# Convolutional attention and an expert layer on one core: idle transposes ahead of the first tokens, and the order of steps as a table

## The chip, the cores and the metric

The kernel runs on one core of a Trainium2 chip. The metric is the device time of one execution in microseconds (us); lower is better. The engines of the core are called PE (TensorE, the matrix engine; PEld is its loading of weights), DVE (VectorE), ACT (ScalarE), POOL (GpSimd) and SP (SyncE, which here only issues transfers). Each takes its instructions in program order.

## What is computed

Two stages on 33280 tokens of 192 numbers. First a causal convolution whose seven taps are a softmax per token and head:

```python
w = softmax(weight_gen)                       # [8, 4160, 8 heads, 7 taps]
x_unf = the last 7 rows of x for each token   # zeros ahead of the start
out = einsum('bshk,bskhg->bshg', w, x_unf)    # 8 heads x 24 numbers
```

Then an expert layer on the result `x` (33280 x 192), with `w_in` 192 x 1024 and `w_out` 1024 x 192:

```python
h = x @ w_in
solu = h * softmax(h)
ln = (solu - mean) / sqrt(var + 1e-6) * g_ln
return ln @ w_out
```

## The kernel before

**Tiling.** 33280 tokens are 128 partitions of 260 consecutive tokens. The kernel walks the 260 token indices t; one "tile" is the 128 tokens with the same t. x and the tap weights are loaded in chunks (token indices 0 to 3, 4 to 11, then 16 at a time).

**Steps.** The work is cut into 4199 named steps, each with the token index it works on. For one tile:

- POOL: `attA` (line 191) multiplies x by the tap weights for two tiles (up to token 11) or four tiles at once into the buffer `pr` (four buffers); `attB` (206) adds some of the seven products to each other; `t1` (109) and `t6` (122) prepare a chunk's tap weights together with `t0`, `t3`, `t5` on DVE (107, 115, 120) and `t2`, `t4` on ACT.
- The remaining parts are summed either by PE, which transposes each part and accumulates (`xT`, line 491, one buffer `pa`), or by DVE in `fin` (477), after which `xT` transposes the sum. The first twelve tiles leave all or nearly all parts to PE: 21 transposes per pair.
- `xhi` (ACT, 501) and `xld` (DVE, 505) copy the transposed pair out of `pa` as a high and a low half in f16; `sw` (SP, 511) makes a copy with the halves swapped.
- `mm1` (PE, 526 and 534) is the first product, six narrow pairs and six wide matmuls, into one of three buffers `h`. `max` (DVE, 556), `exp` (ACT, 562), `solu` (DVE, 570), `sq` (ACT, 576), `hi` (ACT, 583), `lo` (DVE, 587) work on it; `lo` is the last reader of `h`. `tr` (SP, 595) transposes the f16 halves by DMA.
- `mm2` (PE, 635) is the second product, 24 matmuls; `out` (ACT, 646) scales it, `od` stores four tiles. `f0` to `f5` make the layer norm's scale once per four tiles.

**Start-up.** The weights arrive as the two words of doubles. `a`, `b` steps turn `w_in` into f32 (lines 274 to 290), `c` steps `w_out`. `n0`, `n1`, `n2` (ACT, 328) sum the squares of `w_in`, `n4` (PE, 335) adds the sums over the partitions, `n6` and `n7` make a scale of it, `a03` to `b4` scale the weights into f16, and `w0` (SP, 307 to 311) copies them into a second arrangement for odd tiles; then `mm1` can start. `q` and `p` steps scale and centre `w_out` for `mm2` (`q.0` on POOL, 379; `p8` on DVE, 428). `v` steps make a norm of x per chunk. `x0` (248) masks the first rows, `lx` and `lw` load the chunks from the third on, `lx` in four parts.

**The idle products.** `pw` (`run_ahead`, 250 to 253) is PE's first step: 44 matmuls of fp32 ones with the first chunk of x, into `pa`, of which nothing is read. The `xT` of the first pair follows it on PE.

**The order.** `plan` lists each step with its engine, a cost and the steps that it waits for; `issue_order` then plays the plan engine by engine and at each turn takes the ready step with the smallest number, token index plus an entry of `URGENCY`. The instructions are written in that order, and each engine keeps it:

```python
for op, t in issue_order(plan(RUN, starts, group, stat_group, LOADS, parts)):
    ops[op](t)
```

Of the kernel before, what the change touches and what calls it, by code (L numbers as in the profile page):

```python
# [26 lines left out]
def tile_kernel(ctx: ExitStack, tc: tile.TileContext, x, weight_gen, w_in, w_out, g_ln, out):  # L27
    nc = tc.nc
    P = 128
# [95 lines left out]


# [123 lines left out]
    def run_ahead():  # L250
        pa = ps_a.tile([P, 3, P], F32, name="pa")
        for _ in range(AHEAD):
            nc.tensor.matmul(pa[:, 0, :D2], ones, xs[0][:, HALO * D : HALO * D + D2], start=True, stop=True)  # L253
# [109 lines left out]

# [234 lines left out]

# [100 lines left out]
    for op, t in issue_order(plan(RUN, starts, group, stat_group, LOADS, parts)):  # L699
        ops[op](t)  # L700

URGENCY = dict(
    a00=230.54, a01=-169.86, a02=78.81, a03=-71.26, a04=-52.3, a05=-245.39, a06=20.39, a10=-199.02,
    a11=183.38, a12=139.02, a13=75.55, a14=-236.05, a15=8.56, a16=-231.01, attA=(-80.23, 0, 0, 0),
    attA_0=93.55, attA_10=178.99, attA_2=-38.93, attA_4=125.32, attA_6=21.36, attA_8=6.86,
    attB=(58.83, 0, 0, 0), attB_0=40.66, attB_10=-53.52, attB_2=-167.73, attB_4=27.22, attB_6=-4.54,
    attB_8=126.24, b0=158.76, b1=-174.19, b2=200.95, b3=244.46, b4=-122.49, b5=232.43, b6=77.77,
    c00=-206.66, c01=-92.96, c02=162.77, c05=204.94, c06=-171.28, c10=-58.15, c11=-212.47,  # L710
    c12=49.83, c15=212.2, c16=242.46, c20=190.09, c21=97.28, c22=-4.95, c25=136.4, c26=-31.36,
    exp=(-145.96, -219.37, 18.21, 132.23), exp_0=197.26, exp_1=237.51, exp_10=83.17, exp_11=-194.86,
    exp_2=-108.44, exp_3=174.98, exp_4=36.04, exp_5=44.51, exp_6=-71.15, exp_7=57.6, exp_8=-99.33,
    exp_9=226.63, f0=(0, 0, 0, 153.51), f0_11=-38.19, f0_3=404.55, f0_7=96.61, f1=(0, 0, 0, 45.43),
    f1_11=224.73, f1_3=57.21, f1_7=-131.49, f2=(0, 0, 0, 256.79), f2_11=-171.14, f2_3=167.13,
    f2_7=-230.92, f3=(0, 0, 0, -162.74), f3_11=-141.49, f3_3=4.68, f3_7=-10.02, f4=(0, 0, 0, 5.77),
    f4_11=200.54, f4_3=174.19, f4_7=104.74, f5=(0, 0, 0, -199.21), f5_11=182.08, f5_3=193.17,
    f5_7=-182.31, fin=(115.66, 0, 69.89, 0), hi=(61.88, -187.14, -241.68, -119.88), hi_0=-28.29,
    hi_1=-69.46, hi_10=-154.42, hi_11=188.61, hi_2=234.68, hi_3=-165.38, hi_4=58.97, hi_5=32.18,
    hi_6=-155.21, hi_7=148.5, hi_8=53.7, hi_9=-126.75, lo=(-195.34, -225.17, -19.45, -178.56),  # L720
    lo_0=-73.26, lo_1=165.75, lo_10=-179.95, lo_11=-185.1, lo_2=-144.88, lo_3=-74.94, lo_4=228.22,
    lo_5=35.88, lo_6=-187.55, lo_7=-24.94, lo_8=-124.22, lo_9=-91.39, lw=-14.78, lx0=-135.21,
    lx1=125.55, lx2=223.55, lx3=-66.11, max=(-67.16, -31.06, -160.3, -253.27), max_0=-6.63,
    max_1=-109.95, max_10=-2.35, max_11=-181.02, max_2=-173.74, max_3=137.03, max_4=202.43,
    max_5=109.99, max_6=-231.43, max_7=-121.9, max_8=204.82, max_9=-131.88, mm1=(-241.67, -119.54,
    -126.73, 78.79), mm1_0=-129.22, mm1_1=194.49, mm1_10=216.67, mm1_11=108.18, mm1_2=-55.59,
    mm1_3=-173.16, mm1_4=-181.37, mm1_5=-116.52, mm1_6=99.99, mm1_7=119.82, mm1_8=-217.85,
    mm1_9=218.56, mm2=(-76.61, -1.63, 161.38, -206.56), mm2_0=59.48, mm2_1=-155.68, mm2_10=243.66,
    mm2_11=-207.18, mm2_2=-130.59, mm2_3=-13.88, mm2_4=40.87, mm2_5=-249.66, mm2_6=183.99,
    mm2_7=107.74, mm2_8=61.49, mm2_9=-113.27, n0=39.48, n1=53.35, n2=38.52, n4=201.04, n6=203.48,  # L730
    n7=-33.93, od=(0, 0, -76.55, -133.12), od_11=174.52, od_3=60.29, od_7=79.7, out=(-153.63, 6.11,
    53.99, -124.59), out_0=30.56, out_1=-87.51, out_10=-73.71, out_11=228.15, out_2=-278.7,
    out_3=212.6, out_4=2.25, out_5=-245.97, out_6=46.29, out_7=-69.48, out_8=-146.66, out_9=-22.02,
    p30=-79.19, p31=-243.38, p4=191.82, p5=174.62, p6=333.78, p70=25.49, p71=-226, p80=-73.8,
    p81=-140.51, p9=-85.22, pw=-76.84, q00=-128.77, q01=29.8, q02=27.49, q10=69.29, q11=242.54,
    q12=-155.16, q20=170.97, q21=339.47, q22=156.26, q30=228.51, q31=-227.09, q32=128,
    solu=(-199.24, -182.01, 8.5, -14.44), solu_0=129.39, solu_1=-56.22, solu_10=230.35,
    solu_11=-117.79, solu_2=99.72, solu_3=150.7, solu_4=-164.75, solu_5=118.7, solu_6=32.69,
    solu_7=-85.43, solu_8=22.47, solu_9=-24.22, sq=(81.8, -245.34, -58.76, 192.06), sq_0=192.25,
    sq_1=-73.99, sq_10=91.57, sq_11=62.94, sq_2=210.83, sq_3=7.36, sq_4=129.68, sq_5=-193.11,  # L740
    sq_6=-205.04, sq_7=-44.39, sq_8=-223.66, sq_9=-123.3, sw=(55.97, 0, 163.95, 0), sw_0=-167.4,
    sw_10=-118.23, sw_2=36.54, sw_4=39.41, sw_6=112.6, sw_8=-212.75, t0=271.79, t0_0=42.36,
    t0_4=216.57, t1=124.99, t1_0=-52.31, t1_4=-202.08, t2=245.01, t2_0=-82.33, t2_4=62.1, t3=136.26,
    t3_0=57.54, t3_4=69.25, t4=-31.14, t4_0=-142.07, t4_4=-84.48, t5=234.35, t5_0=-56.17,
    t5_4=-172.56, t6=94.73, t6_0=149.42, t6_4=97.15, tr=(-72.45, -45.15, 237.8, -222.84),
    tr_0=233.38, tr_1=48.73, tr_10=85.22, tr_11=40.86, tr_2=139.35, tr_3=109.02, tr_4=-170.49,
    tr_5=-176.28, tr_6=107.6, tr_7=43.11, tr_8=-31.21, tr_9=-152.72, v00=82.2, v00_0=198.87,
    v00_4=224.23, v01=218.42, v01_0=-245.65, v01_4=-75.77, v02=129.37, v03=233, v1=116.62,
    v1_0=-126.67, v1_4=-222.18, v2=226.63, v2_0=-231.41, v2_4=-20.17, v3=49.62, v3_0=-71.33,
    v3_4=35.56, v4=239.66, v4_0=-195.81, v4_4=113.57, v5=-56.74, v5_0=-173.27, v5_4=-127.37,  # L750
    w0=209.28, x0=-211.37, xT=(-87.23, 0, 53.04, 0), xT_0=77.08, xT_10=-226.06, xT_2=-99.19,
    xT_4=-107.64, xT_6=91.42, xT_8=-169.15, xhi=(-90.84, 0, -70.56, 0), xhi_0=165, xhi_10=188.48,
    xhi_2=152.35, xhi_4=-22.69, xhi_6=134.05, xhi_8=-231.09, xld=(44.29, 0, 58.42, 0), xld_0=-215.1,
    xld_10=-25.58, xld_2=124.15, xld_4=-166.69, xld_6=-122.65, xld_8=83.12,
)
# [18 lines left out]
LOADED = 20500  # L774
AHEAD = 44
CENTRED = 3
# [8 lines left out]
SUMS = {2: 880, 3: 1380, 4: 1840, 5: 2300}  # L785
LATER = dict(max=40, solu=35, mm1=0, mm2=95)


def plan(run, starts, group, stat_group, loads, parts):

    PE, DVE, ACT, SP, POOL = range(5)
    steps = []

    def add(name, t, engine, cost, *after, ready=0):
        steps.append((name, t, engine, cost, [x for x in after if x[1] >= 0], ready))

    def once(name, engine, cost, *after, ready=0):
        add(name, 0, engine, cost, *((x, 0) for x in after), ready=ready)

    def chunk_of(t):  # L800
        return max(c for c in range(len(starts) - 1) if starts[c] <= t)

    weights = dict(a0=8900, a1=10700, b=12500, c0=16200, c1=17500, c2=19200)
    order = list(weights)
    for n, part in enumerate(order):
        at = weights[part]
        sized = [order[n - 1] + "1"] if n else []
        if n > 3:
            sized.append(order[n - 4] + "2")
        once(part + "1", ACT, 620, *sized, ready=at)  # L810
        once(part + "0", DVE, 715, ready=at)
        once(part + "5", DVE, 715, part + "0")
        once(part + "6", DVE, 715, part + "5")
        once(part + "2", DVE, 700, part + "6", part + "1")
        if n < 3:
            once({"a0": "n0", "a1": "n1", "b": "n2"}[part], ACT, 830, part + "2")
            once(part + "3", ACT, 580, part + "2", "n7")
            once(part + "4", DVE, 660, part + "3")
    once("w0", SP, 3600, "a04", "a14", "b4")
    for f, part in enumerate(("c0", "c1", "c2", "c2")):  # L820
        made = (["c02"], ["c02", "c12"], ["c12", "c22"], ["c22"])[f]
        once(f"q{f}0", POOL, 830, *made, ready=16000)
        once(f"q{f}1", PE, 660, f"q{f}0", f"q{f - 1}1" if f else "c02")
        once(f"q{f}2", ACT, 520, f"q{f}0", "n4")
    for half, old in enumerate(centred_after()):
        add(f"p3{half}", 0, DVE, 900, ("q31", 0), ("mm1", CENTRED), *([("p30", 0)] if half else []), *old)
# [13 lines left out]
    def last_group(c):  # L840
        if c < 0:
            return ("attA", -1)
# [260 lines left out]
```

## Time and profile before

| | us |
|---|---|
| median of 3 runs | 1234.22 (1233.54 to 1234.49) |
| the profiled execution | 1234.71 |
| its span, first to last instruction | 1232.9 |
| PE, DVE, ACT, POOL busy | 1197.4, 1162.3, 1124.0, 1134.8 |

The profile is one execution. Its span lies 1.8 us below the execution's own time. A row of a timeline gives the start of a group of instructions, its length, engine, line, operation, what it writes and reads, and in brackets the idle time ahead of it with what ended it. Matmul ends are modelled, so neighbouring rows of PE overlap a little.

### The profile page before, as it was taken

The numbers are of one execution on the slowest core, as the hardware profiler recorded it, in microseconds if no ns is written. First come the engines' busy times: TensorE is split into PE (matmuls) and PEld (weight loads), VectorE is DVE, ScalarE is ACT, GpSimd is POOL, SyncE is SP. The second block draws the span as 40 slices with busy tenths as digits, with TensorE's granted clock in tenths as the row PEclk, the third lists the DMA queues.
The fourth block names the chain that finished last, engine by engine and source line by source line (L and its number), as shares of the span: only waits on it lengthen the run. The fifth ranks groups of instructions, "written<-read, shape, count | busy, mean of one in ns | idle before, by whom it ended". The sixth has DMA issues, their size and how long they took to land.

```text
span 1232.9 us, 27480 instructions
## 1 busy us (share of the span) xinstructions
PE 1197.4 (97%) x10303; PEld 829.2 (67%) x10303; DVE 1162.3 (94%) x1814; ACT 1124.0 (91%) x2295; POOL 1134.8 (92%) x243
## 2 busy tenths in 40 slices
PE   7899999999999999999999999999999999999998
PEld 7666666666666666666676666666666666666666
DVE  5989999999999999999999999999999999988994
ACT  4899898999899898999989999999999999999985
POOL 6689999999999999999999999999999999999930
PEclk9999999999999999999999999999999999999999
DMA  6787889989797988989698999979899897987786
GB/s 202 157 188 146 200 156 210 178 183 182 164 210 153 225 165 170 192 174 213 138 220 175 186 185 169 203 150 231 161 188 184 178 195 145 195 161 150 152 150 129
DMA packets 586069, 219.19 MB, mean 178 GB/s; under 512 B 548624, under 2 KB 566288, under 8 KB 585935
## 3 DMA queue, kind: packets, MB, share of 16 engines
q1 hardware_dynamic: 585776, 216.84, 86.1%
q8 instruction: 81, 1.33, 0.5%
q10 hardware_dynamic: 158, 0.59, 0.1%
q14 instruction: 54, 0.43, 0.1%
HBM read 46.19 MB, written 25.56 MB: 58 GB/s over the span
## 4 chain that ended last, share of the span: by engine, by line
ACT 35%; DVE 24%; PE 23%; issue 12%; DMA 5%; SPq 1%; ACTq 0%; DVEq 0%
ACT e L576 10%; PE po L635 9%; ACT hl L583 8%; ACT e L562 8%; DVE h L556 8%; PE h L534 7%; DVE h L570 6%; DVE hl L587 5%; PE h L526 4%; ACT junk L156 2%; DVE a L477 2%; ACT ot L646 2%; DMA xt<-in_x_dram 2%; PE pa L491 2%; PE pa L253 2%
## 5 line engine op out<-in xcount | busy, mean ns | idle before, releaser
L191 POOL TENSOR_TENSOR pr<-xt,wt 128x5376 f32<-128x5376 f32 (+1 forms) x68 | 631.3, 9284 | 0.9
L635 PEld LDWEIGHTS <-hlT 128*128 128x128 f16 x6240 | 522.5, 98 | 52.0 <-issue 7.9
L635 PE MATMUL po<-w_hl,hlT 128*128 128x192 f16 x6168 | 550.9, 246 | 5.5 <-ACT ot L646 5.4
L206 POOL TENSOR_TENSOR pr<-pr 128x2304 f32<-128x2304 f32 (+2 forms) x128 | 445.7, 3482 | 9.3
L570 DVE SCALAR_TENSOR_TENSOR h<-h,row,e 128x1024 f32<-128x1024 f32 x260 | 333.5, 1284 | 7.3 <-ACT e L562 4.2
L587 DVE SCALAR_TENSOR_TENSOR hl<-h,hl 128x1024 f16<-128x1024 f32 x260 | 311.3, 1216 | 28.0 <-ACT hl L583 17.1
L556 DVE TENSOR_SCALAR_CACHE_REDUCE h<-h,row 128x1024 f32<-128x1024 f32 x260 | 334.0, 1285 | 3.9 <-PE h L534 3.1
L562 ACT ACTIVATE e<-h,stats 128x1024 f32<-128x1024 f32 x260 | 294.9, 1134 | 38.2 <-DVE h L556 26.8
L576 ACT ACTIVATE e<-h,stats 128x1024 f32<-128x1024 f32 x260 | 294.4, 1134 | 30.3 <-DVE stats L607 24.9
L534 PEld LDWEIGHTS <-xh 128*128 128x128 f16 x1560 | 131.3, 98 | 234.5 <-issue 109.8
L583 ACT ACTIVATE hl<-h 128x1024 f16<-128x1024 f32 x260 | 268.7, 1034 | 4.8 <-DVE h L570 4.0
L534 PE MATMUL h<-wa,xh 128*128 128x512 f16 x780 | 190.9, 381 | 1.6 <-DVE wa L353 1.6
L534 PE MATMUL h<-oa,xh 128*128 128x512 f16 x780 | 191.0, 381 | 0.0
L646 ACT ACTIVATE ot<-po,stats 128x192 f32<-128x192 f32 x257 | 114.1, 444 | 5.1 <-PE po L635 4.6
L526 PE MATMUL h<-ob,turned 64*128 64x512 f16 x390 | 106.1, 378 | 10.3 <-DVE hl L587 9.1
L526 PE MATMUL h<-wb,xh 64*128 64x512 f16 x390 | 106.8, 380 | 3.6 <-DVE hl L587 3.0
L526 PE MATMUL h<-wb,turned 64*128 64x512 f16 x390 | 106.4, 380 | 0.8 <-DMA turned<-xh 0.8
L526 PE MATMUL h<-ob,xh 64*128 64x512 f16 x390 | 106.4, 380 | 0.6 <-DMA ob<-wa 0.6
L477 DVE TENSOR_REDUCE a<-pr 128x384 f32<-128x1152 f32 (+1 forms) x58 | 86.4, 1491 | 0.0
L491 PE MATMUL pa<-ident,pr 128*128 128x128 f32 x651 | 84.7, 276 | 1.4 <-DVE xh L505 1.2
L526 PEld LDWEIGHTS <-xh 64*128 64x128 f16 x780 | 53.6, 94 | 46.7 <-issue 24.7
L491 PEld LDWEIGHTS pa<-ident,pr 128*128 128x128 f32 x651 | 76.1, 143 | 12.8 <-issue 2.1
(91 smaller groups left out, 892.6 us busy)
## 6 DMA issues: line engine op xcount, KB each, us to landing
out_dram<-ot SPq DMA_DIRECT2D x64, 384.0 KB, 3.2
xt<-in_x_dram SPq DMA_DIRECT2D x30, 576.0 KB, 4.9
xt<-in_x_dram SPq DMA_DIRECT2D x30, 480.0 KB, 4.5
turned<-xh SPq DMA_DIRECT2D x260, 32.0 KB, 2.2
wt<-in_weight_gen_dram SPq DMA_DIRECT2D x15, 448.0 KB, 5.4
hlT<-hl SPq DMA_TRANSPOSE x260, 4.8
hlT<-in_moe_w_out_dram SPq DMA_DIRECT2D x3, 512.0 KB, 8.9
xt<-in_x_dram SPq DMA_DIRECT2D x3, 384.0 KB, 4.2
```

Of the source, the lines that this page charges most:

```text
L191: nc.gpsimd.tensor_tensor(out=window(pr, 0, [(ROW, K), (HG, n * H), (1, HG)]), in0=window(xt, t * D, [(D, K), (HG, n * H), (1, HG)]), in1= ...
L206: nc.gpsimd.tensor_tensor(out=b, in0=b, in1=a, op=ALU.add)
L491: nc.tensor.matmul(pa[:, k], source[:, first : first + P], ident, is_transpose=True, start=at == 0, stop=at == 3 * len(sources) - 1,)
L526: nc.tensor.matmul(h[:, fs], last[(f + odd) % 2][rows, low], b[rows, which], start=start and n == 0, stop=stop and n == 2,)
L534: nc.tensor.matmul(h[:, fs], xh[:, 2 * odd, low], a[:, which, fs], start=start and n == 0, stop=stop and n == 2,)
L556: nc.vector.tensor_scalar(h, h, row(t, BACK), 3.0e38, op0=ALU.mult, op1=ALU.min, accum_out=stat(t, NMAX))
L562: nc.scalar.activation(e, h_of[t], AF.Exp, bias=stat(t, NMAX), scale=-1.0, accum_out=stat(t, Z))
L570: nc.vector.scalar_tensor_tensor(out=h, in0=h, scalar=row(t, SCALE), in1=e, op0=ALU.mult, op1=ALU.mult, accum_out=stat(t, M))
L576: nc.scalar.activation(e_of.pop(t), h_of[t], AF.Square, bias=stat(t, M), scale=-float(FF), accum_out=stat(t, Q),)
L583: nc.scalar.activation(hl[:, 0, :], h_of[t], AF.Copy, scale=2.0**14)
L587: nc.vector.scalar_tensor_tensor(out=hl[:, 1, :], in0=h_of[t], scalar=2.0**14, in1=hl[:, 0, :], op0=ALU.mult, op1=ALU.subtract,)
L635: nc.tensor.matmul(po[:, :D], hlT[:, half * NJ + j, :], w2_hl[:, j, w, :], start=n == 0, stop=n == len(terms) - 1,)
```

## The change

Two things. `pw` no longer multiplies: it transposes the first 128 columns of the same x tile against the identity, 56 times instead of 44, into the same unread buffer. And the order of all steps is written down: one letter names a step, `ORDER` is the string of 4199 signs, letters and 67 dots, a dot for each step that occurs once (their names are in `ONCE`), and the k-th occurrence of a letter is that step for its k-th token index. `plan`, the costs and `URGENCY` are gone. The set of the 4199 steps and what each of them does are otherwise the same, but the order is not that of before.

```diff
     def run_ahead():
         pa = ps_a.tile([P, 3, P], F32, name="pa")
         for _ in range(AHEAD):
-            nc.tensor.matmul(pa[:, 0, :D2], ones, xs[0][:, HALO * D : HALO * D + D2], start=True, stop=True)
+            nc.tensor.matmul(
+                pa[:, 0], xs[0][:, HALO * D : HALO * D + P], ident, is_transpose=True, start=True, stop=True
+            )
...
-AHEAD = 44
+AHEAD = 56
...
-    for op, t in issue_order(plan(RUN, starts, group, stat_group, LOADS, parts)):
+    for op, t in issue_order({name: times.get(name, tokens) for name in STEPS}):
         ops[op](t)
...
+STEPS = dict(
+    v5="0", f0="A", f1="B", f2="C", f3="D", f4="E", f5="F", lw="G", lx0="H", lx1="I", lx2="J",
+    lx3="K", t0="L", t1="M", t2="N", t3="O", t4="P", t5="Q", t6="R", v00="S", v01="T", v02="U",
+    v03="V", v1="W", v2="X", v3="Y", v4="Z", attA="a", attB="b", od="d", exp="e", mm1="h", hi="i",
+    lo="l", max="m", fin="n", mm2="o", sq="q", tr="r", solu="s", out="u", sw="w", xT="x", xhi="y",
+    xld="z",
+)
+ONCE = (
+    "pw a00 x0 a05 a06 a10 a01 a15 a11 b0 b1 a16 b5 a12 b6 a02 n1 n0 c10 b2 c01 c15 n2 c20 c25 "
+    "c11 c16 n4 c26 n6 c21 n7 a13 c22 a03 a14 b3 a04 b4 c00 w0 c12 c05 q30 c06 q20 q22 q32 c02 "
+    "q10 q00 q12 q02 q01 q11 q21 q31 p30 p31 p5 p6 p70 p80 p9 p71 p4 p81 "
+)
+ORDER = (
+    "LMNHGTO.S..W.X..P.Q.R.a.....S.T..L..Mx..baNW...XO....Py..z..QxwI..R...ba.YY.y.h.Zz.wSJG.m."
...
```

The orders of the first steps on PE, read off both (the table's below the old one):

```
before: pw xT(0) n4 xT(2) mm1(0) xT(4) q01 mm1(1) mm1(2) xT(6) mm1(3) q11 q21 q31 xT(8) p5 xT(10) mm1(4) mm1(5) mm2(0)
after:  pw xT(0) n4 xT(2) mm1(0) xT(4) mm1(1) mm1(2) mm1(3) q01 q11 xT(6) q21 q31 xT(8) p5 mm1(4) xT(10) mm1(5) mm2(0)
```

On POOL the old order begins `t1(0) t6(0) attA(0) t1(4) attA(2) t6(4) attA(4) q00 q30 attA(6) q10 q20 attA(8) t1(12) attA(10) t6(12)`, the table's `t1(0) t6(0) attA(0) t1(4) attA(2) t6(4) attA(4) q30 q20 t1(12) q10 q00 attA(6) attA(8) attA(10) t6(12)`.

## Rows read from the trace of the kernel before

**Rows 1.** The page's head: span, and busy time of each engine.

```profile
span 1232.9 us, 27480 instructions
PE 1197.4 (97%) x10303; PEld 829.2 (67%) x10303; DVE 1162.3 (94%) x1814; ACT 1124.0 (91%) x2295; POOL 1134.8 (92%) x243
```

**Rows 2.** Waits of PE from 36 us on: total us, times, longest.

```profile
PE h L526 <- DVE hl L587: 12.1, 28, 1.1
```

**Rows 3.** Timeline of PE, first 65 us: start, length, instructions, idle before.

```profile
6.96 19.01 PE L253 MATMUL pa<-xt,ones 128*128 128x64 f32 x88 [6.96 <-DMA xt<-in_x_dram]
26.12 4.16 PE L491 MATMUL pa<-ident,pr 128*128 128x128 f32 x21
30.11 0.73 PE L335 MATMUL h<-sq,ones 128*128 128x1 f32 x6
...
35.61 1.46 PE L534 MATMUL h<-wa,xh 128*128 128x512 f16 x6 [1.59 <-DVE wa L353]
...
41.86 0.37 PE L526 MATMUL h<-ob,xh 64*128 64x512 f16 x1 [0.63 <-DMA ob<-wa]
...
42.60 1.47 PE L534 MATMUL h<-oa,xh 128*128 128x512 f16 x6
...
64.86 2.14 PE L635 MATMUL po<-w_hl,hlT 128*128 128x192 f16 x24
```

**Rows 4.** Timeline of POOL, first 65 us.

```profile
12.04 4.94 POOL L191 TENSOR_TENSOR pr<-xt,wt 128x2688 f32<-128x2688 f32 x1
...
23.82 4.94 POOL L191 TENSOR_TENSOR pr<-xt,wt 128x2688 f32<-128x2688 f32 x1
33.84 0.82 POOL L379 TENSOR_TENSOR a<-a,g 128x384 f32<-128x384 f32 x1 [5.08 <-DVE a L290]
...
64.60 1.75 POOL L122 TENSOR_TENSOR wt<-wt,wy 128x896 f32<-128x896 f32 x1 [9.00 <-DVE wy L120]
```

**Rows 5.** Timelines of ACT and of DVE around 20 to 31 us.

```profile
20.62 0.20 ACT L328 ACTIVATION_READ_ACCUMULATOR junk<-h 128x1 f32 x1
...
30.31 0.48 ACT L501 CAST xh<-pa 128x384 f16<-128x384 f32 x1 [9.17 <-PE pa L491]
...
30.83 0.56 DVE L505 TENSOR_TENSOR xh<-pa,xh 128x384 f16<-128x384 f32 x1 [8.56 <-ACT xh L501]
```

**Rows 6.** PE by line in 20:24, 27:29, 30:30.5: count, busy us, mean ns.

```profile
L253 PE MATMUL pa<-xt,ones 128*128 128x64 f32 x20 | 4.5, 421 | 0.0
...
L491 PE MATMUL pa<-ident,pr 128*128 128x128 f32 x11 | 2.6, 417 | 0.0
...
L491 PE MATMUL pa<-ident,pr 128*128 128x128 f32 x3 | 0.5, 273 | 0.0
```

**Rows 7.** Stretches, line 491 alone: us, PE, PEld busy (starts), granted clock, DMA.

```profile
26.06:28.00 1.94, 1.88 (x9) 1.91 (x10) 1.00 0.03 8
31.50:34.00 2.50, 2.47 (x21) 2.27 (x21) 1.00 0.29 45
```

**Rows 8.** Timelines of POOL and PE: products done and taken, tokens 12 and 252.

```profile
77.81 3.45 POOL L206 TENSOR_TENSOR pr<-pr 128x1536 f32<-128x1536 f32 x1
...
85.29 1.80 PE L491 MATMUL pa<-ident,pr 128*128 128x128 f32 x15
...
1151.95 10.47 POOL L206 TENSOR_TENSOR pr<-pr 128x2304 f32<-128x2304 f32 x3
...
1164.29 0.49 PE L491 MATMUL pa<-ident,pr 128*128 128x128 f32 x3
```

**Rows 9.** Timelines of DVE and PE: `xld(16)` and `xT(18)`, `xld(20)` and `xT(22)`.

```profile
107.40 0.55 DVE L505 TENSOR_TENSOR xh<-pa,xh 128x384 f16<-128x384 f32 x1
...
109.89 1.47 PE L491 MATMUL pa<-ident,pr 128*128 128x128 f32 x12
...
120.37 0.55 DVE L505 TENSOR_TENSOR xh<-pa,xh 128x384 f16<-128x384 f32 x1
...
125.09 1.47 PE L491 MATMUL pa<-ident,pr 128*128 128x128 f32 x12
```

More of the change, by code (lines that the diff above doesn't have):

```diff
@@ L1 @@
-import heapq
 from contextlib import ExitStack
@@ L696, in tile_kernel @@
         ops[f"t{n}"] = at_chunk(softmax_taps, n)
-    for op, t in issue_order(plan(RUN, starts, group, stat_group, LOADS, parts)):
-        ops[op](t)
[L704 to L755, printed above, removed]
@@ new lines, in tile_kernel @@
+    tokens, pairs, heads = range(RUN), range(0, RUN, 2), starts[:-1]
+    times = dict(
+        attA=[t for t in tokens if group(t)], fin=[t for t in pairs if not parts(t)[1]],
+        od=[t for t in tokens if t % TG == TG - 1 or t == RUN - 2],
+    )
+    times["attB"] = times["attA"]
+    for name in ("xT", "xhi", "xld", "sw"):
+        times[name] = pairs
+    for n in range(6):
+        times[f"f{n}"] = [t for t in tokens if stat_group(t)]
+    for name in ("lw", *(f"lx{n}" for n in range(LOADS))):
+        times[name] = starts[2:-1]
@@ L758 @@
+    for name in (*(f"v{n}" for n in range(1, 6)), *(f"t{n}" for n in range(TAP_STEPS))):
+        times[name] = heads
+    for n in range(4):
+        times[f"v0{n}"] = [
+            t for c, t in enumerate(heads) if 4 * n < starts[c + 1] - t or (c == 0 and n == 1)
+        ]
+    for op, t in issue_order({name: times.get(name, tokens) for name in STEPS}):
+        ops[op](t)
 PARTS = ((3, (True, False)), (3, (True, False)), (3, (True, False)), (3, (True, False)), (3, (True, False)), (3, (True, False)), (3, (True, False)), (3, (False,)))
@@ L771, in parts_of @@
     return count, on_tensor[t % size // 2 % len(on_tensor)]
-LOADED = 20500
-AHEAD = 44
-CENTRED = 3
+AHEAD = 56
 GROUPS = 4
@@ L962, in readers @@
-def readers(u):
-    scratch = (["a04", "a14"], ["b4", "n6"], ["c12", "c22"])
-    if isinstance(u, str):
-        return [("p8" + u[1], 0)]
-    if u < 0:
-        return [(name, 0) for name in scratch[u + 3]]
-    return [("sq", u), ("lo", u)]
-def in_turn():
-    k = CENTRED + 1
-    return [-3, -2, -1, *range(k), "c0", "c1", *range(k, k + 6)]
-def centred_after():
-    turn = in_turn()
-    return [readers(turn[turn.index(c) - 3]) for c in ("c0", "c1")]
-def held(t):
-    turn = in_turn()
-    return readers(turn[turn.index(t) - 3] if t in turn else t - 3)
@@ L988 @@
-MARGIN = {
[3 rows of a table removed]
-}
-def issue_order(steps):
-    PE, DVE, ACT, SP, POOL = range(5)
-    SAME, CROSS, FROM_PE = (25, 127, 143, 0, 102), 130, 200
-    free = [2000, 5000, 4500, 6500, 4500]
-    number = {(name, t): i for i, (name, t, *_) in enumerate(steps)}
-    then, count, ready = [[] for _ in steps], [0] * len(steps), [s[5] for s in steps]
-    for i, step in enumerate(steps):
-        for name, t, *early in step[4]:
-            then[number[name, t]].append((i, *early))
-            count[i] += 1
-    def urgency(name, t):
-        u = URGENCY.get(f"{name}_{t}", URGENCY.get(name, 0))
-        return u[t % 4] if isinstance(u, tuple) else u
-    key = [round(t + urgency(name, t), 6) for name, t, *_ in steps]
-    later, now = [[] for _ in free], [[] for _ in free]
-    for i, step in enumerate(steps):
-        if not count[i]:
-            heapq.heappush(later[step[2]], (ready[i], key[i], i))
-    def gap(step, to):
-        e, on = step[2], to[2]
-        late = MARGIN.get((step[0][:2], to[0][:2]), 0) if to[1] > 11 else 0
-        if e == on and on != SP:
-            return SAME[e] + late
-        return (FROM_PE if e == PE and on != SP else CROSS) + late
-    queue, data = 0, LOADED
-    busy = warm = -10000
-    order = []
-    while True:
-        able = [
-            (free[e] if now[e] else max(free[e], later[e][0][0]), e)
-            for e in range(len(free)) if now[e] or later[e]
-        ]
-        if not able:
-            break
-        time, e = min(able)
-        while later[e] and later[e][0][0] <= time:
-            _, k, i = heapq.heappop(later[e])
-            heapq.heappush(now[e], (k, i))
-        k, i = heapq.heappop(now[e])
-        if ready[i] > time:
-            heapq.heappush(later[e], (ready[i], k, i))
-            continue
-        name, t, _, cost, *_ = steps[i]
-        order.append((name, t))
-        free[e] = time + cost
-        end = free[e] + LATER.get(name, 0)
-        if e == PE:
-            if time - busy > 2000:
-                warm = time + 3400
-            if time < warm:
-                slow = time + 2 * cost if time + 2 * cost < warm else (time + warm) / 2 + cost
-                free[e], end = slow, end + slow - free[e]
-            busy = free[e]
-        if e == SP:
-            queue = max(queue, time) + (655 if name == "tr" else 500)
-            data = max(queue + 400, data) + cost
-            free[e], end = time + 60, data + 870
-        if name in ("sq", "lo"):
-            j = number["lo" if name == "sq" else "sq", t]
-            ready[j] = max(ready[j], free[e] + CROSS)
-        for j, *early in then[i]:
-            ready[j] = max(ready[j], end + gap(steps[i], steps[j]) - sum(early))
-            count[j] -= 1
-            if not count[j]:
-                heapq.heappush(later[steps[j][2]], (ready[j], key[j], j))
-    assert len(order) == len(steps)
@@ L1067, in issue_order @@
+def issue_order(times):
+    name_of = {letter: name for name, letter in STEPS.items()}
+    left = {name: iter(times[name]) for name in STEPS}
+    once = iter(ONCE.split())
+    order = []
+    for letter in ORDER:
+        if letter == ".":
+            order.append((next(once), 0))
+        else:
+            name = name_of[letter]
+            order.append((name, next(left[name])))
+    assert all(next(each, None) is None for each in (*left.values(), once))
     return order
```

208 lines of the change are left out of this document (48 added, 160 removed), and 3 rows, old and new, of the table MARGIN.

## The prediction

> **What bounds the kernel now.** I read the page's shares first, then the waits of TensorE (PE), then the first 65 us engine by engine, then how far the producers run ahead of PE late in the run. PE is busy for 97% of the span, VectorE (DVE) 94%, GpSimd (POOL) 92% [rows 1]: three engines are nearly full, so a microsecond won on one of them counts only if the other two move by as much. After 36 us PE's largest loss is 12.1 us in 28 waits, in which `mm1` finds its score buffer still read by `lo` of three tokens earlier, a DVE step [rows 2]; all its listed waits there come to about 22 us. So after the start there is no large hole to close. The large hole is at the start.
>
> There PE runs the idle products of `pw` from 6.96 for 19.01 us, and the first real transpose block, `xT(0)`, begins only at 26.12 [rows 3]. Its input, the product of the first pair of tokens, was finished by POOL at 12.04 + 4.94 = 16.98 [rows 4]. PE works in order, so `xT(0)` stood behind the idle products for 9.1 us. ACT had its last start-up sum ready at 20.62 + 0.20 = 20.82, then sat idle for 9.17 us until `xT(0)` was through, and DVE sat idle for 8.56 us for the same reason [rows 5]. PE, ACT and DVE thus have one and the same hole of about 9 us.
>
> **The change part by part.** *The idle block.* 44 fp32 products, which are 88 records on PE, go; 56 transposes come. The new ones have the shape of `xT`'s (128x128 fp32, one record each), so `xT` prices them. While the idle products ran, a record took 421 ns and held that value for 19 us; the first `xT` transposes after them took 417 ns, and those after 30 us took 273 ns [rows 6]. In spacing: nine starts in 1.94 us at first (0.216 us each), 21 in 2.47 us later (0.118) [rows 7]. The granted clock is printed as 1.00, the 2.4 GHz level, in both stretches [rows 7], so here I go by the durations: slow through the products and for some 3.4 us of transposes (26.1 to 29.5), fast after that. What PE did before the rise was transposes, back to back; the products had not brought it about in 19 us. Prices for the 56, then: all slow 56 x 0.216 = 12.1 us (end 19.1), all fast 6.6 us (end 13.6); with the rise after 3.4 us, 16 slow and 40 fast ones, 3.4 + 40 x 0.118 = 8.1 us. I take the last, as it repeats what `xT(0)` did: the block ends at 15.1. It is then hidden under POOL's product, which ends at 16.98. If the rise comes late, up to 2 us of it stick out.
>
> The Trainium skill, TensorE: Matmul & The Clock Gate, Part 4: PE-mode transpose, says that the full clock does not engage for transposes, because they do not count as a busy PE in the same way. By that rule every transpose ahead of the first product would stay slow. The trace speaks against it, with 417 ns falling to 273 ns inside a run of nothing but transposes [rows 6].
>
> *The first tokens.* `xT(0)` starts at 17.1 and takes 2.5 us: 19.6, against 30.28 before. The next step on PE, `n4` (30.11 before [rows 3]), needs three sums of squares; the last ended at 20.82 [rows 5]. In the order of before that gives 20.9, so 9.2 us earlier. In the new table DVE does the bits of `b` ahead of `c00` and `c20`, which brings that sum to about 19.5 by the same durations, but ACT gets `c11`, `t4(4)` and `xhi(0)` between it and `n6`. From there the old chain to `mm1(0)` (30.11 to 35.61 [rows 3]) is kept. So `mm1(0)` starts 9.2 to 9.9 us earlier. `mm1(1)` waited for the odd-row weights that five SP copies bring after `b4` (41.86 [rows 3]); these copies follow the weights, so it moves along.
>
> *POOL* is not moved at first: its products start at 12.04 in both. `t1(4)` now stands behind a later `t0(4)`, and `t6(4)` behind a later `t5(4)`, so the second product ends near 22.9 and the third near 29.4 instead of 28.76. PE waits for both, the third ahead of `mm1(1)`; that fits under the weight copies. But POOL then loses its 5 us wait for `c02` (23.82 + 4.94 to 33.84), and `t1(12)` and all four `q` steps go ahead of the remaining pairs: 29.4 + 4 x 0.82 + 1.75 + three products of 4.95 and about 1 us of waits end near 50, where the sixth product ended at 64.60 - 9.00 = 55.60; 9.00 is what `t6(12)` then waited for DVE [rows 4]. DVE's work ahead of it is the same and its hole is gone, so it comes about 9.5 us earlier, at 55. Then the products of token 12 are done 16.7 us later (64.60 to 81.26), near 72, and PE asks for them at 85.29 - 9.5 = 75.8 [rows 8]. PE is not stopped.
>
> *SP.* `lw(28)` goes behind `lx2(12)`, and `lx3(12)` behind `tr(0)`, which waits for `lo(0)`. Ahead of `lx3`'s reader, `v03(12)` on ACT, lie three tiles of `exp`, `sq` and `hi`, about 10 us; the load needs some 5. Nothing on PE waits for it.
>
> *The middle.* On PE 196 of 657 steps have another place, nearly all by one neighbour; on DVE 802 of 1287. Work and instructions are the same. From token 12 on, 38 `xT` blocks go ahead of an `mm2` or `mm1`. There is one `pa` buffer, so `xT(t)` must follow `xld(t-2)` on DVE. In 12 of the 38 the old distance is smaller than the work that is overtaken: from `xT(18)`, which started 2.0 us after the end of `xld(16)` and now passes 7.2 us of work, to `xT(22)`, 4.2 us against 4.4 [rows 9]. The 12 shortfalls sum to 24 us. That is the upper bound of a loss. In eleven of the 12 the table moves `xld(t-2)` ahead on DVE as well, and in the twelfth, `xT(28)`, the sum `fin(28)` that it reads. The bound of a gain is PE's 22 us of waits. Between these ends I take nothing, since neither the work nor the kind of wait changes.
>
> *The end.* POOL's last groups are short of slack: the products of group 252 end at 1151.95 + 10.47 = 1162.42 and PE takes them at 1164.29, 1.9 us later [rows 8]. PE can gain at most POOL's gain plus 1.9. With 5.5 us on POOL (its sixth product alone) that would be 7.4; with 9.5 it binds nothing.
>
> **Sum.** 9.5 us (between 9.2 and 9.9). The profiled execution took 1234.71 us, its span 1232.9; less 9.5 this is 1225.2. The median of the three runs, 1234.22, is 0.5 lower: 1224.7. A measurement of this kernel tells some 0.2%, 2.5 us, from no change.
>
> **Rivals.**
> 1. *The clock stays down for the idle transposes.* They end at 19.1, `xT(0)` takes 4.5 us, `n4` starts at 23.7 instead of 30.11, and the first two `mm1` cost about 2 us more: a gain of 4 to 6, 1229.5. Against it: rows 6. This is what the skill's sentence would give. 6%.
> 2. *The clock falls again in the gaps.* PE will now wait for POOL from 15.1 to 17, and from 20.3 to 22.9. If it goes slow there, `xT(2)` takes 4.5 us instead of 2.5, and `mm1(0)` and the blocks after it lose 1 to 2 more: 1228. For it: no gap that long lies in PE's first 65 us after 30. Against it: after the 1.59 us of idle ahead of `mm1(0)` its six wide products took 1.46 us, as long as the 1.47 of the next `mm1` [rows 3]. 10%.
> 3. *Slower: the single `pa` buffer.* Each `xT` that was put ahead waits for `xld`, with `mm1` and `mm2` queued behind it on PE. Price 24 us if no `xld` comes sooner: 1225 + 24 = 1249. It makes the kernel slower only if more than 40% of it is paid, 9.5 of 24. Against it: the `xld` steps move along. 4%.
> 4. *The gain is given back.* POOL or DVE is no earlier by token 252, and PE then waits where it did not: 1232 to 1234. Against it: both have the hole or its cause at the start. 6%.
> 5. *The new order also removes waits.* A third of the 22 us would give 1217.5. For it: the waits on `lo` depend on the order alone. 17%.
>
> **The numbers.** The forecast has 57%, with 1222 to 1228 as its own range. Rivals 1 and 2 reach to 1230, rival 5 to 1217; 1218 to 1230.5 leaves out rivals 3 and 4, the far half of 5 and little else. Faster by over 0.2%: the forecast and rivals 1, 2 and 5, and part of 4: 0.92. Same: most of rival 4: 0.04. Slower: rival 3: 0.04.
>
> **What would show it.** Right: 56 records of the idle block in about 8 us, at 417 ns and then 273; `xT(0)` at 17; no hole of 9 us on ACT or DVE; `mm1(0)` near 26, `mm2(0)` near 55; PE's waits after that still near 22 us, with `lo` at their head. Wrong: records of 417 ns up to `mm1(0)` (rival 1), `xT(2)` over 4 us (rival 2), many PE waits on `xh` of line 505 (rival 3), PE waits on POOL or a much longer list of `lo` waits (rival 4).

## The result, and the profile after

The changed kernel takes 1216.24 us (median; 1216.01 to 1216.69), the one before 1234.36 beside it: a ratio of 0.9854, 95% interval 0.9837 to 0.9872, 18.1 us less. The forecast was 1224.7, with a range from 1218.0. The direction was right and the start came out nearly as worked out; the gain is twice the forecast, because the order of the steps brought about as much again as the shorter idle block.

The start after the change, in the timeline of PE (start, length, engine, line, operation, count, idle before):

```profile
7.14 8.31 PE L250 MATMUL pa<-ident,xt 128*128 128x128 f32 x56 [7.14 <-DMA xt<-in_x_dram]
17.18 2.51 PE L489 MATMUL pa<-ident,pr 128*128 128x128 f32 x21 [1.72 <-POOL pr L188]
19.52 0.81 PE L334 MATMUL h<-sq,ones 128*128 128x1 f32 x6
23.01 2.51 PE L489 MATMUL pa<-ident,pr 128*128 128x128 f32 x21 [2.67 <-POOL pr L188]
25.75 1.45 PE L532 MATMUL h<-wa,xh 128*128 128x512 f16 x6 [0.23 <-DVE wa L352]
...
56.06 2.14 PE L632 MATMUL po<-w_hl,hlT 128*128 128x192 f16 x24
```

Each row answers to one of [rows 3]. The idle block is 8.3 us long instead of 19.0, `xT(0)` starts at 17.18 instead of 26.12, `mm1(0)` at 25.75 instead of 35.61 (9.9 us earlier), and the first `mm2` at 56.06 instead of 64.86. PE now waits for POOL's products, as its brackets say. PE by line within the idle block, from 9 to 10.5 us and from 12 to 15 us (count, busy us, mean ns):

```profile
L250 PE MATMUL pa<-ident,xt 128*128 128x128 f32 x9 | 2.1, 421 | 0.0
...
L250 PE MATMUL pa<-ident,xt 128*128 128x128 f32 x30 | 3.4, 273 | 0.0
```

The transposes start at the slow pace of [rows 6] and end at the fast one.

The same stretch in the timeline of POOL:

```profile
12.18 4.94 POOL L188 TENSOR_TENSOR pr<-xt,wt 128x2688 f32<-128x2688 f32 x1
...
24.48 4.94 POOL L188 TENSOR_TENSOR pr<-xt,wt 128x2688 f32<-128x2688 f32 x1
...
34.85 14.75 POOL L188 TENSOR_TENSOR pr<-xt,wt 128x2688 f32<-128x2688 f32 x3
54.13 1.75 POOL L121 TENSOR_TENSOR wt<-wt,wy 128x896 f32<-128x896 f32 x1 [4.52 <-DVE wy L119]
```

The third product is 0.7 us later than in [rows 4], as forecast, the sixth ends at 49.6 instead of 55.6, and the step after it waits 4.52 us instead of 9.00.

The surprise is in the rest of the run. The waits of PE from 50 us on (total us, times, longest):

```profile
PE h L524 <- DVE hl L585: 4.7, 12, 1.1
PE po L632 <- ACT ot L643: 4.6, 6, 1.8
PE h L524 <- DMA turned<-xh: 1.2, 2, 0.8
```

The waits of `mm1` on `lo` are 4.7 us in 12, where [rows 2] had 12.1 in 28. The part of the page on the chain that ended last shows a larger shift. Before and after:

```profile
ACT 35%; DVE 24%; PE 23%; issue 12%; DMA 5%; SPq 1%; ACTq 0%; DVEq 0%
```

```profile
PE 53%; DVE 22%; ACT 9%; issue 9%; DMA 3%; SPq 0%; DVEq 0%; ACTq 0%
```

Before, the chain ran through ACT for a third of the span and through PE for less than a quarter, although PE was 97% busy: by this view the end hung more on the ring `max`, `exp`, `solu`, `hi`, `lo` between DVE and ACT than on PE. After, the chain is mostly PE. ACT's waits say the same, from 60 us on. Before:

```profile
ACT e L562 <- DVE h L556: 25.0, 27, 1.8
ACT e L576 <- DVE stats L607: 24.9, 32, 1.6
ACT e L562 <- DVE stats L607: 11.3, 14, 1.1
```

After:

```profile
ACT e L560 <- DVE h L554: 11.1, 25, 1.7
ACT hl L581 <- DVE h L568: 8.4, 19, 1.3
ACT e L574 <- DVE hl L585: 6.0, 13, 1.3
ACT e L560 <- DVE stats L604: 5.3, 12, 0.9
ACT hl L581 <- DVE stats L604: 5.1, 8, 1.4
```

ACT's three largest waits on DVE came to 61.2 us before; the five largest after come to 35.9.

PE does the same work in both kernels, so its idle time tells what the order won. From `mm1(0)` to the last `mm1`, first before, then after (us, PE busy, then the other engines):

```profile
35.61:1209.18 1173.57, 1152.83 (x9963) 786.73 (x9964) 1133.81 (x1759) 1093.52 (x2221) 1115.41 (x228) 1.00 0.88 179
```

```profile
25.75:1190.41 1164.66, 1151.85 (x9963) 785.02 (x9964) 1136.42 (x1761) 1103.12 (x2226) 1119.29 (x230) 1.00 0.90 180
```

PE stood idle for 20.7 us of it before and for 12.8 after. These 7.9 us are most of the 8.9 by which the stretch became shorter.

Where the 18.7 us of span went (1232.9 to 1214.2) can be laid out by three starts in the timelines of PE: `mm1(0)` at 35.6 before and 25.75 after, `mm1(24)` at 152.5 and 138.1, the last `mm1` at 1209.2 and 1190.4. For `mm1(24)`, before and after:

```profile
152.45 0.39 PE L526 MATMUL h<-wb,xh 64*128 64x512 f16 x1 [0.55 <-DVE hl L587]
```

```profile
138.06 0.39 PE L524 MATMUL h<-wb,xh 64*128 64x512 f16 x1
```

Up to `mm1(0)` the gain is 9.9 us; from there to `mm1(24)` 4.5 (116.8 against 112.3); from `mm1(24)` to the last `mm1` 4.4 (1056.7 against 1052.4); from there to the end nothing (23.7, 23.8).

### The profile page after: what moved, and what is told of

Same layout as the page of the kernel before. It is cut to its first block, busy times and chain, and to the rows that moved or that the text cites. A ratio compares the mean times of both kernels' runs of the same rounds, so it can differ in the third digit from the quotient of the medians.

```text
span 1214.2 us, 27274 instructions
## 1 busy us (share of the span) xinstructions
PE 1184.2 (98%) x10271; PEld 815.1 (67%) x10271; DVE 1164.1 (96%) x1814; ACT 1133.9 (93%) x2295; POOL 1134.2 (93%) x243
## 4 chain that ended last, share of the span: by engine, by line
PE 53%; DVE 22%; ACT 9%; issue 9%; DMA 3%; SPq 0%; DVEq 0%; ACTq 0%
PE po L632 23%; PE h L532 17%; PE h L524 9%; DVE h L554 7%; DVE hl L585 6%; DVE h L568 5%; PE pa L489 4%; ACT e L560 3%; ACT hl L581 3%; ACT e L574 2%; DVE a L475 1%; DVE xh L503 1%; DMA turned<-xh 1%; DMA xt<-in_x_dram 1%; ACT ot L643 1%
## 5 line engine op out<-in xcount | busy, mean ns | idle before, releaser
L585 DVE SCALAR_TENSOR_TENSOR hl<-h,hl 128x1024 f16<-128x1024 f32 x260 | 313.5, 1217 | 10.8 <-ACT hl L581 5.1
L581 ACT ACTIVATE hl<-h 128x1024 f16<-128x1024 f32 x260 | 265.8, 1033 | 16.0 <-DVE h L568 8.4
L643 ACT ACTIVATE ot<-po,stats 128x192 f32<-128x192 f32 x257 | 110.4, 430 | 10.4 <-PE po L632 7.4
L489 PEld LDWEIGHTS pa<-ident,pr 128*128 128x128 f32 x651 | 73.5, 141 | 15.4 <-POOL pr L188 7.6
L524 PEld LDWEIGHTS <-turned 64*128 64x128 f16 x780 | 54.3, 94 | 40.6 <-issue 22.6
```

The lines of the kernel that those rows point to most:

```text
L489: nc.tensor.matmul(pa[:, k], source[:, first : first + P], ident, is_transpose=True, start=at == 0, stop=at == 3 * len(sources) - 1,)
L524: nc.tensor.matmul(h[:, fs], last[(f + odd) % 2][rows, low], b[rows, which], start=start and n == 0, stop=stop and n == 2,)
L581: nc.scalar.activation(hl[:, 0, :], h_of[t], AF.Copy, scale=2.0**14)
L585: nc.vector.scalar_tensor_tensor(out=hl[:, 1, :], in0=h_of[t], scalar=2.0**14, in1=hl[:, 0, :], op0=ALU.mult, op1=ALU.subtract,)
```

## The experiments

All ratios are against the kernel before on the same chip.

**Old order, new idle block.**

```diff
-            nc.tensor.matmul(pa[:, 0, :D2], ones, xs[0][:, HALO * D : HALO * D + D2], start=True, stop=True)
+            nc.tensor.matmul(
+                pa[:, 0], xs[0][:, HALO * D : HALO * D + P], ident, is_transpose=True, start=True, stop=True
+            )
-AHEAD = 44
+AHEAD = 56
```

> The old order, with 56 idle transposes in place of the 44 products. Theory (the start and the order give their gains separately): the block ends near 15.3, xT(0) starts near 17.1, mm1(0) about 9.2 us earlier than before, and the waits of PE after that stay near 20 us with lo at 12: 1234.4 - 9.2 = 1225. Rival A (the shorter waits after the start come from the earlier start, not from the order): waits of PE near 10 us, 1217. Rival B (the old order cannot use the earlier xT(0)): 1232 or more.

Measured: 1226.58 us, ratio 0.9936 (0.9921 to 0.9951). `mm1(0)` began at 26.70, 8.9 us earlier than before, as the theory had it, and the waits after the start stayed. PE and ACT, from 50 us on, and the shares of the chain that ended last:

```profile
PE h L528 <- DVE hl L589: 11.6, 27, 1.1
...
ACT e L578 <- DVE stats L609: 24.8, 32, 1.6
ACT e L564 <- DVE h L558: 24.7, 27, 1.4
```

```profile
ACT 38%; DVE 27%; PE 16%; issue 14%; DMA 4%; SPq 1%; ACTq 0%; DVEq 0%
```

So neither the shorter waits nor the shift of the chain come from the earlier start. Rivals A and B both fall.

**Table, old idle block.** The table with line 250 of before and `AHEAD = 44`.

> The table, with the 44 idle products of before. Theory: xT(0) near 26.2 again and mm1(0) near 35, but the waits of PE after the start stay near 10 us: 1216.2 + 9.3 = 1225.5. Rival A (the order only works with the earlier start): waits near 20 us, 1234.

Measured: 1223.17 us, 0.9908 (0.9894 to 0.9923), 2.3 us less than expected. `xT(0)` was back at 26.03, and PE's waits on `lo` were 2.5 us in 8. The chain is PE's, as in the changed kernel:

```profile
PE 47%; DVE 26%; ACT 12%; issue 10%; DMA 3%; SPq 1%; POOL 0%; DVEq 0%; ACTq 0%; POOLq 0%
```

The two parts add up to about the whole: 7.9 us for the block alone and 11.3 for the order alone, 19.2 together, against 18.1 for both at once. Each of these is uncertain by some 2 us.

**Which idle block.** The table with 19 of the products of before (line 250 as in the last experiment) in one kernel, with no idle block in the other:

```diff
-AHEAD = 56
+AHEAD = 19
```

```diff
-AHEAD = 56
+AHEAD = 0
```

> The table, with 19 idle products: a block of the same length (8.2 us) as the 56 transposes, but of the kind that ran at 421 ns throughout. Theory (only the transposes bring the fast clock): xT(0) begins at 17.1 and takes some 4.2 us instead of 2.5, n4 is 1.7 later, xT(2) still waits for POOL until 23; if xT(0) has made it fast by then mm1(0) is at most 1 us later: 1216 to 1217.5. Rival (the length of the block is all that matters): xT(0) takes 2.5 us.

> The table, with no idle block at all. Theory: as with 19 products, since these do not raise the clock: xT(0) at 17.1 with 417 ns a transpose for 3.4 us, 4.2 us in all, 1216 to 1217.5. Rival (an idle block of any kind is needed, the clock rises late without one): mm1(0) 2 us or more later, 1218.5 or above.

Measured: 1214.51 us with 19 products, 0.9834 (0.9817 to 0.9851); 1217.90 with none, 0.9864 (0.9849 to 0.9878). The intervals of both overlap that of the changed kernel. The first lies 1.5 us below its expected range, the second 0.4 above it. With 19 products, PE:

```profile
7.17 8.34 PE L250 MATMUL pa<-xt,ones 128*128 128x64 f32 x38 [7.17 <-DMA xt<-in_x_dram]
17.20 4.07 PE L487 MATMUL pa<-ident,pr 128*128 128x128 f32 x21 [1.69 <-POOL pr L188]
...
23.04 2.51 PE L487 MATMUL pa<-ident,pr 128*128 128x128 f32 x21 [1.20 <-DVE unit_w L341]
26.14 1.46 PE L530 MATMUL h<-wa,xh 128*128 128x512 f16 x6 [0.59 <-DVE wa L350]
```

As expected, the products leave `xT(0)` at the slow pace (4.07 us), and `xT(2)` is fast. It costs `mm1(0)` 0.4 us, and nothing of that can be measured at the end. With no block at all the slow pace lasted longer than expected: `xT(0)` took 4.74 us, `xT(2)` still 4.17, and `mm1(0)` began at 27.11, 1.4 us later than in the changed kernel. The rival there had asked for 2 us or more and 1218.5. The two kernels lie 3.4 us apart and their intervals barely touch, so a small cost of having no block is not excluded. What counted in the first half of the change is that the block now ends before POOL's first product does; whether it is made of transposes or of products did not matter.

**Spliced orders.** Both have the 56 transposes; the whole order was written out step by step, a prefix of one order and then the remaining steps in the other. From here on the lines marked - and + name steps in their order and are not lines of the file.

```diff
-table
+table up to mm1(24), then the remaining steps as before
...
-before
+before up to mm1(24), then the remaining steps as in the table
```

> 56 idle transposes; the steps in the table's order up to mm1(24), the rest in the old order. Theory (the table's gain sits in many places, part of it in tiles 4 to 24, part later): mm1(24) some 14 us earlier than before as in the table's own run, and after it the old pitch, with the waits on lo near 10 us: 1219 to 1220.5. Rival A (all of the order's gain is in the start): 1216. Rival B (all of it is later): 1226, as with the old order throughout.

> 56 idle transposes; the steps in the old order up to mm1(24), the rest in the table's. Theory: mm1(24) some 7.5 us earlier than before, as with the old order and the transposes, then the table's shorter waits add some 5: 1221 to 1223. Rival A (the gain is in the start): 1226. Rival B (it is later): 1216.

Measured: 1222.30 us, 0.9903 (0.9888 to 0.9918), and 1222.74 us, 0.9903 (0.9886 to 0.9919). PE's waits on `lo` from 50 us on, first the splice with the old order behind, then the one with the table behind:

```profile
PE h L524 <- DVE hl L585: 11.4, 27, 1.0
```

```profile
PE h L524 <- DVE hl L585: 5.7, 12, 1.1
```

The waits follow the order that is in force. From `mm1(24)` to the last `mm1` the two took 1058.1 and 1051.5 us (138.3 to 1196.4, and 148.5 to 1200.0); kernels with the old order throughout 1055.0 and 1056.7, with the table 1050.5 to 1054.9. The first splice missed its expected time by 2 us: I had counted the old order's later part about 2 us too short. The second met its time. Its trace is of the slowest of its four executions (1225.54 us), and there the start lost about 3.5 us more than in the kernel it was reckoned from, `mm1(24)` being 4.0 us earlier than before instead of 7.5. PE had the odd-row weights only at 35.70, where the first experiment had them at 33.88, and its clock had fallen behind that wait (below). Both rivals fall: the order's gain lies in the tiles up to 24 and in the later part, about half and half.

**The changed kernel again, and the table with SP's old order.** PE, DVE, ACT and POOL keep the table's order; SP alone issues its transfers in the old one.

```diff
-SP: lx1(12) w0 sw(2) lx2(12) lw(28) sw(4) tr(0) lx3(12)
+SP: lx1(12) lw(28) w0 lx2(12) sw(2) sw(4) lx3(12) tr(0)
```

> The changed kernel itself, on the chip of the three splices, as what they are set against: 1214.5 to 1217.

> The table, with SP alone in the order of before (loads, stores, DMA transposes, swaps); PE, DVE, ACT and POOL as in the table. Theory (the gain comes from the order of PE, DVE and ACT among each other): 1215.5 to 1218. Rival (it comes from DMA transposes that go ahead of stores and tap loads on SP): back by 4 us or more, 1220 and above.

Measured: the table again 1216.51 us, 0.9855 (0.9840 to 0.9869), as expected; with SP's old order 1235.54 us, 1.0014 (1.0002 to 1.0025). The whole gain is gone, so my theory was wrong on the time. But not by the rival's mechanism. Waits of PE from 50 us on:

```profile
PE h L524 <- DMA turned<-xh: 11.5, 8, 3.0
PE po L632 <- ACT ot L643: 4.4, 6, 1.8
PE h L524 <- DVE hl L585: 4.1, 10, 1.1
```

The wait on `lo` stayed short, at 4.1 us. In its place `mm1` waits for the swapped halves of x. In six of the eight waits the old SP order has the swap (`sw`) right behind a DMA transpose (`tr`), which in its turn waits for the compute engines: ahead of `mm1(134)`, the longest of them, SP stood at a `tr` from 646.1 to 650.2 us, while the half to be swapped was there at 647.8. All listed waits of PE from 50 us on come to 23.2 us, against 9.5 when the table was run again. PE's clock was lower too, 0.993 in the mean against 0.999, so the waits are not the whole of the 19 us.

**The reverse: old order, SP alone as in the table.**

```diff
-SP: lx1(12) lw(28) w0 lx2(12) sw(2) sw(4) lx3(12) tr(0)
+SP: lx1(12) w0 sw(2) lx2(12) lw(28) sw(4) tr(0) lx3(12)
```

> The old order with 56 idle transposes, SP alone in the table's order; PE, DVE, ACT and POOL as before. Theory (each engine's order is fitted to the others', SP's to its own compute engines): waits of mm1 on the swapped halves or of mm2 on the DMA transposes appear, 1229 to 1240. Rival A (the table's SP order is good by itself): 1220 to 1224. Rival B (SP has slack, its order is free): 1226 to 1227.

Measured: 1246.80 us, 1.0103 (1.0086 to 1.0120), 20 us more than the old order with its own SP order. The table's SP order is not good by itself, and both rivals fall. The theory had the direction, but not the size, nor the kind of wait: the waits on the swapped halves are 3.1 us in 4. New are those for `out` on PE and for the chunk loads on ACT:

```profile
PE po L632 <- ACT ot L643: 15.7, 14, 2.9
...
ACT junk L153 <- DMA xt<-in_x_dram: 13.7, 6, 3.3
```

**`lo` ahead of `max`.** Of the 40 `mm1` from tile 15 to 249 that began within 0.12 us of the end of `lo` in the trace before, 33 had the same pattern on DVE: `solu(u+1)`, `max(u+2)`, then `lo(u)`, for which `mm1(u+3)` waited. In the old order with the transposes these 33 were turned round:

```diff
-DVE: ... solu(47) max(48) lo(46) ...
+DVE: ... solu(47) lo(46) max(48) ...
```

> The old order with 56 idle transposes (1226.6), changed on DVE alone in 33 places: there lo(u) stood behind solu(u+1) and max(u+2), and mm1(u+3) on PE waited for it; now lo(u) goes ahead of max(u+2). In 32 of the 33, hi(u), which lo(u) reads, was done when max(u+2) began. Theory (PE's waits on lo come from these places): the waits on lo fall from 11.6 us to some 4, 1219 to 1222. Rival (the loss goes on to max and exp, which are 1.2 us later in those places): lo's waits fall, other waits rise by as much, 1225 to 1228.

Measured: 1278.75 us, 1.0362 (1.0346 to 1.0377), 52 us slower than without it. The theory's time is far off, and the rival was far too mild. PE, DVE and ACT from 50 us on:

```profile
PE po L632 <- ACT ot L643: 52.6, 69, 1.4
PE h L524 <- DVE hl L585: 8.1, 17, 1.0
...
DVE hl L585 <- ACT e L574: 43.9, 55, 1.8
...
ACT e L560 <- DVE h L554: 78.0, 60, 1.7
```

PE's wait on `lo` fell from 11.6 to 8.1 us. But `exp` on ACT now waits 78.0 us for the later `max` (24.7 without the edit), ACT works in order, so `out` behind it is late, and `mm2` waits 52.6 us for `out` (3.5 without). DVE itself waits longer as well, 43.9 us ahead of `lo` (10.3 without), and the instruction that it waits for is `sq` on ACT. The expectation had looked at `hi(u)` alone. But `sq(u)` and `lo(u)` read the same buffer `h`, and in the 14 traces of this case, with 260 tiles each, they never run at the same time; which of them goes first follows the order of the steps. The edit left `sq(u)` ahead of `lo(u)`. In 32 of the 33 places the moved `lo(u)` began 0.12 to 0.13 us after the end of `sq(u)`, when `hi(u)` had been done for 1.1 us or more. So DVE stood still ahead of `lo`, and `max` came later by that as well. This run is therefore no clean test of whether the place of `lo` costs PE its waits.

**The place of `fin`.** In the old order with the transposes 49 `fin` sums were put behind the neighbour that they have in the table, and the other way round in the table.

```diff
-DVE: ... max(105) f1(103) fin(114) lo(104) ...
+DVE: ... max(105) f1(103) lo(104) fin(114) ...
```

> The old order with 56 idle transposes, and on DVE alone the fin sums from tile 24 on behind the same neighbour as in the table (49 of them in another place, mostly later by one to three steps). Theory (the place of the 1.4 us fin decides whether lo is late): waits on lo from 11.6 to 5 or 6 us, 1221 to 1223. Rival (the fins have no part in it): 1226 to 1227.5.

> The table, and on DVE alone the fin sums from tile 24 on behind the neighbour they had in the old order. Theory (the place of fin decides): waits on lo from 4 or 5 us to 10, 1220 to 1222. Rival (no part): 1215.5 to 1217.5.

Measured: 1252.23 us, 1.0142 (1.0127 to 1.0157), and 1255.25 us, 1.0177 (1.0160 to 1.0194): 26 and 39 us more than the kernels that they came from. The first row is of the old order with the new places, the second of the table with the old ones:

```profile
PE h L524 <- DVE hl L585: 27.1, 44, 2.1
```

```profile
PE po L632 <- ACT ot L643: 20.3, 23, 2.1
```

Neither the theory nor the rival had expected that. The place of `fin` by itself does not bring the table's gain, and each of the five exchanges on a single engine made the order that it was made in worse.

## Why the prediction was right or wrong

- *The idle block* was right: 8.3 us instead of 8.1, slow for its first records (421 ns) and fast at its end (273 ns), and hidden under POOL's first product. In the ten traces with the 56 transposes it takes 7.6 to 9.1 us.
- *The first tokens* were right: `mm1(0)` 9.9 us earlier, the upper end of the 9.2 to 9.9. With the old order alone it was 8.9.
- *POOL* was right to within 1 us: third product 29.4, sixth 49.6 against 50, `t6(12)` at 54.1 against 55. PE was not stopped by it later.
- *SP* was costed at nothing, and in the table it is next to nothing (1.2 us of waits on the swapped halves, 0.8 before). But the runs with exchanged SP orders show 19 and 20 us: it is hidden only because SP's order was changed together with the others.
- *The middle* is the step that failed: "Between these ends I take nothing, since neither the work nor the kind of wait changes." It measured 8.9 us (4.5 up to `mm1(24)`, 4.4 after), and 11.3 us with the order alone. The bound of the gain, PE's 22 us of waits, held: from 50 us on PE's listed waits came to 21.6 us before and to 11.0 after. What had no support was the value between the bounds: that the work and the kind of wait stay the same says nothing about how long the waits are, since these depend on the order. With the same steps, the runs with exchanged orders moved the time by 19 to 52 us. The profile held signs that the order was tight, which the prediction did not read: the chain that ended last with ACT at 35% and PE at 23%, and 61 us of ACT's waits on DVE.
- *Rival 5* is what happened: the order removed waits, those on `lo` first (4.7 us instead of 12.1). It had 17%, and its price, a third of the 22 us and 1217.5, was a little low.
- *Rival 1* did not occur. *Rival 2* did not in the profiled execution, but it did in most other traces (last section): that `xT(2)` took 2.51 us here was luck. In the table it cost nothing that could be measured, so its price of 3 us was too high. *Rival 3*, the single `pa` buffer, did not occur in the table: PE's waits on `xld` from 50 us on are 0.2 us. *Rival 4* did not: token 252's part of the run keeps the gain.
- *The range* left out the far half of rival 5, where the result lies, 1.8 us below the lower end.

What stays open is which exchanges within the table bring the 8.9 us. The orders of PE, DVE and ACT hang on each other, so that exchanging a whole one of the three leaves a step waiting for itself in a circle; that was not tried, and POOL's order was not exchanged alone either. The three partial exchanges on DVE did not tell it, since each upset more than it mended. One difference lies in the traces: `lo(u)` goes ahead of `sq(u)` in 70 of the 260 tiles in the old order and in 134 in the table, and DVE's idle time ahead of `lo` (after the last bar) fell from 28.0 us to 10.8:

```profile
L587 DVE SCALAR_TENSOR_TENSOR hl<-h,hl 128x1024 f16<-128x1024 f32 x260 | 311.3, 1216 | 28.0 <-ACT hl L583 17.1
```

```profile
L585 DVE SCALAR_TENSOR_TENSOR hl<-h,hl 128x1024 f16<-128x1024 f32 x260 | 313.5, 1217 | 10.8 <-ACT hl L581 5.1
```

It may be part of the cause, but no run changed it alone, and it is not enough: the table with the old places of `fin` has 129 such tiles, and DVE idles 30.5 us there. That the gain is one of the joint order is shown; its division among engines is not.

## What to carry to other kernels

The idle time of the busiest engine bounds what an order can win, here PE's 22 us; to take nothing of it needs a reason as much as to take all. Read the chain that ended last beside the busy shares: PE was 97% busy, and yet the chain ran mostly through two other engines, whose waits a new order could shorten. The orders of engines that work in order belong together: taking one engine's order, or one step's place, from a better order into a worse one, or back, cost 19 to 52 us here, while the whole table won 11. Before moving a step ahead, look at every step that shares a buffer with it, the readers too. Filler work ahead of the first real work must end before that work's input is there; here its length was worth 8 us, and its kind nothing that could be measured.

## What the runs showed of the hardware

PE's clock did fall again in the gaps at the start, where PE waits mostly for POOL, in most traces and not in all, even for the same kernel. Of the ten traces with the 56 transposes ahead, `xT(2)` took 2.51 us in three and 3.85 to 4.74 in seven. In the changed kernel's first profile it took 2.51 us. When it was run again, it took 3.85 after 2.74 us of idle, and the granted clock of 20 to 24 us was 0.75 (between the levels of 1.2 and 2.4 GHz, so slow for half of the stretch):

```profile
22.63 3.85 PE L489 MATMUL pa<-ident,pr 128*128 128x128 f32 x21 [2.74 <-POOL pr L188]
```

```profile
20.00:24.00 4.00, 1.37 (x7) 1.37 (x8) 3.56 (x8) 3.90 (x11) 3.55 (x2) 0.75 0.05 15
```

That execution took 1214.56 us, the first 1216.01. `mm1(0)` began 0.6 us later, at 26.31, but `mm1(1)`, which needs the odd-row weights, at 31.47 against 31.92, so nothing of the slow transposes was left by then. In the second splice PE had waited longer, ahead of `mm1(1)` up to 35.70, for the odd-row weights, and the next six wide products took 2.14 us instead of the usual 1.47, at a granted clock of 0.76:

```profile
36.44 2.14 PE L532 MATMUL h<-oa,xh 128*128 128x512 f16 x6
```

```profile
34.00:40.00 6.00, 4.67 (x19) 1.28 (x19) 2.54 (x6) 2.62 (x5) 6.00 (x4) 0.76 0.55 159
```

The Trainium skill, TensorE: Matmul & The Clock Gate, Part 4: PE-mode transpose, holds that transposes do not bring the full clock. The block of 56 speaks against it: nothing but fp32 transposes ran on PE, and their records went from 421 ns to 273. The products of before did not bring it: in the kernel with 19 of them their records took 421 ns, and `xT(0)` behind them 4.07 us.

`sq` on ACT and `lo` on DVE, which read the same `h`, overlapped in none of the 14 traces: in every tile the second of the two began after the end of the first, by 0.03 us at the least. Whether the chip or the program's own waits keep them apart, no run shows.
